# Moving the last 64 rows of a weight matrix from the start of a decode kernel to its tail, in eight 8-row DMAs, and filling TensorE's waits there

## The chip, the cores and the metric

The kernel runs on one core of a Trainium2 chip. The metric is the device time of one execution in microseconds (us), as the median of several runs. The profile is one more execution under the hardware profiler. Its span, from the first to the last instruction, is some 1.5 us shorter than the device time.

Beside the views that are quoted below, the trace records the start and length of every DMA packet and the arrival of every DMA completion. Neither record names the DMA engine.

## The reference, cut to what matters

One decode step of a transformer layer for four sequences: attention over a cache of 4096 positions, 32 heads of 128, then a small MLP with a Mish activation. Almost all bytes are the K and V caches, each 4 x 32 x 4096 x 128 bf16.

```python
h  = x + attention(layernorm(x), k_cache, v_cache, wq, wo)
h1 = layernorm(h) @ w1 + b1                      # w1: 640 x 1728
y  = h + (h1 * tanh(softplus(h1))) @ w2          # w2: 1728 x 640
```

1728 is 13 blocks of 128 rows and 64 rows over. These last 64 rows of w2, 80 KB, are what the change moves.

## The kernel before

Each engine has its own program, written by hand with semaphores. SyncE issues all large loads. The loads at the start (cut):

```python
def first_loads():
    load(sp, slot["C"][:, 0 : DC * H * Dh], A_wq..., "wq", "WQ")     # 5 MB
    load(ac, x_bf[:, :], x_rows[:, :], "x", "X")                      # ScalarE's queue
    load(ac, w2_tail[0:FT, :], B_w2[FM * P : F, :], "w2t", "WT")      # 64 rows x 1280 B
    k_load(0)                                                         # 8 MB each
    k_load(1)
# ScalarE's program then starts with the two small b1 loads:
    load(ac, b1r..., "b1a", "B0"); load(ac, b1e..., "b1b", "B1")
```

At the end SyncE issues six pieces of wo, three of w1 and four of w2. TensorE's tail (cut) multiplies each piece as it lands:

```python
wo_mm(2); wo_mm(3)                                # last attention projection
pe.need("ysum"); mm(m_ps, ...); pe.need("sq"); mm(sq_ps, ...)         # layernorm sums
pe.need("cen")
for c0, c1 in ((0, 2), (2, 4), (4, 5)):           # three pieces of w1
    pe.need(("w1", c0))
    ...  mm(h1_w[...], w, cen[:, c, :].unsqueeze(1).to_broadcast([P, WD, N]), ...)
pe.need("act")                                    # VectorE, ScalarE: Mish
pe.need("w2t"); w2_mm(FM)                         # the last 64 rows
for j0, j1 in ((0, 4), (4, 8), (8, 12), (12, 13)):
    pe.need(("w2", j0)); ...  w2_mm(j)
```

N is 4, the number of sequences. WD is 16: each vector of four columns is streamed 16 times over, 64 columns, only to keep TensorE busy. The extra 60 columns are thrown away.

The softmax here doesn't subtract the row's maximum and nothing guards it: scores larger than these inputs give would overflow.

## Time and profile before

| | before |
|---|---|
| device time, median of 3 | 661.71 us (661.27 to 662.37) |
| profiled span | 659.9 us |
| bytes moved | 283.48 MB, mean 430 GB/s |
| busy: VectorE, TensorE, ScalarE | 62%, 58%, 6% |
| last two w2 pieces land (completion records) | 656.98 and 657.39 us |

These lines are from the first parts of the profile's page: busy us of each engine, then the span in 40 slices, with the busy share of the 16 DMA engines in tenths and their rate.

```profile
PE 382.4 (58%) x2630; PEld 68.6 (10%) x1672; DVE 407.7 (62%) x257; ACT 40.7 (6%) x157; POOL 1.7 (0%) x12
...
DMA  9999999999999999999999999999999999999997
GB/s 387 445 445 441 434 406 437 442 441 434 430 417 445 437 437 433 437 417 445 433 441 433 437 417 445 433 437 438 433 421 445 429 437 441 433 421 445 415 416 324
DMA packets 6905, 283.48 MB, mean 430 GB/s; under 512 B 809, under 2 KB 1136, under 8 KB 2160
```

No compute engine is near full, but the DMA engines are at nine tenths or more in every slice except the last. The kernel is a stream of 283 MB, and it ends when the last bytes have landed and been used.

The next lines are from the DMA view of the kernel before: destination and source, issuing queue, count, KB each, and us from issue to landing.

```profile
slotC<-in_A_wq_dram SPq DMA_DIRECT2D x1, 5120.0 KB, 16.0
...
w_tail<-in_B_w_dram ACTq DMA_DIRECT2D x1, 80.0 KB, 13.3
```

The chain of waits that ended last, at its end (start, us, what):

```profile
639.18 17.80 DMA slotA<-in_B_w_dram
656.98 0.04 issue
657.02 0.68 PE red L728 x20
657.70 0.02 issue
657.73 0.32 DVE o_bf L724
```

SyncE has issued the piece at 639.18 us, and 17.80 us pass until it lands: it stands behind other loads in the queue. Then come twenty matmuls, a copy and the store. That is all of the tail that is not DMA. By their single records the last four of the twenty start at 657.43 us, 0.04 us after the last piece has landed. So it is the last landing that counts, though the chain names the piece before it.

The timeline of the kernel before, in its last 7 us, with matmul (PE) and VectorE (DVE) lines only; in brackets is the idle time ahead of an instruction and what ended it.

```profile
651.32 1.64 PE L728 MATMUL red<-cen,slotB 128*64 128x64 bf16 x28 [0.78 <-DMA slotB<-in_B_w_dram]
...
652.99 1.08 PE L728 MATMUL red<-cen,slotB 128*64 128x64 bf16 x14
...
655.65 0.22 DVE L717 SCALAR_TENSOR_TENSOR act<-tb,hm 128x56 bf16<-128x56 f32 x1
...
656.09 0.72 PE L728 MATMUL red<-slotA,act 128*4 128x160 bf16 x32
...
657.02 0.65 PE L728 MATMUL red<-slotA,act 128*4 128x160 bf16 x20 [0.21 <-DMA slotA<-in_B_w_dram]
```

TensorE waits for w1 before the first line, and for w2 before the last. The activation (`act`) is ready at 655.87 us, 1.1 and 1.5 us ahead of the last two w2 pieces. The windows view shows TensorE's clock in that tail: busy us of PE, PEld, DVE, ACT and POOL with counts, then granted clock, DMA share and GB/s.

```profile
650.00:652.00 2.00, 1.22 (x31) 1.05 (x28) 0.23 (x3) 0.78 (x1) 0.00 (x0) 0.94 1.03 423
652.00:654.00 2.00, 2.00 (x38) 1.81 (x34) 0.00 (x0) 0.00 (x0) 0.00 (x0) 0.50 1.03 423
654.00:655.00 1.00, 0.83 (x42) 0.64 (x40) 0.74 (x4) 0.25 (x1) 0.00 (x0) 0.50 0.99 396
...
656.00:657.00 1.00, 0.81 (x36) 0.52 (x34) 0.00 (x0) 0.00 (x0) 0.00 (x0) 1.00 0.38 146
```

The clock halves from 652 to 655 us and is full again by the last w2 matmuls.

### The profile page before, as it was taken

Reading aid. Unit: us, or ns where it says so; the run is one execution under the profiler, and the core shown is the slowest. Engines: PE = TensorE matmul, PEld = TensorE weight load, DVE = VectorE, ACT = ScalarE, POOL = GpSimd, SP = SyncE. Lnnn points to the kernel's source line nnn. Section 1 sums busy time; section 2 is a strip of 40 time slices with the busy share of each in tenths; the row PEclk is TensorE's granted clock in tenths of the full one; section 3 lists DMA queues with packets and bytes.
Section 4 is the critical chain, followed back from the end, with each engine's and each line's share of the span. In section 5 each row is a group of like instructions: output and inputs, shape, how many; then the busy total and the mean of one; then the engine's idle time right before and its main releaser. Section 6 shows DMA issues by size and latency. Waiting matters only on the chain. (4 is left out here: it accounts for less than half of the span.)

```text
span 659.9 us, 4968 instructions
## 1 busy us (share of the span) xinstructions
PE 382.4 (58%) x2630; PEld 68.6 (10%) x1672; DVE 407.7 (62%) x257; ACT 40.7 (6%) x157; POOL 1.7 (0%) x12
## 2 busy tenths in 40 slices
PE   0356758556317595738417485848434757675766
PEld 0100000101101010101100010010110001010145
DVE  1077988495049778757208798849306798857702
ACT  0200000000000000000000000000000000000011
POOL 0000000000000000000000000000000000000000
PEclk9768787979759697958767888788875879796968
DMA  9999999999999999999999999999999999999997
GB/s 387 445 445 441 434 406 437 442 441 434 430 417 445 437 437 433 437 417 445 433 441 433 437 417 445 433 437 438 433 421 445 429 437 441 433 421 445 415 416 324
DMA packets 6905, 283.48 MB, mean 430 GB/s; under 512 B 809, under 2 KB 1136, under 8 KB 2160
## 3 DMA queue, kind: packets, MB, share of 16 engines
q1 hardware_dynamic: 6784, 283.27, 99.4%
q8 instruction: 6, 0.10, 0.1%
q10 hardware_dynamic: 112, 0.09, 0.0%
q14 instruction: 3, 0.02, 0.0%
HBM read 283.35 MB, written 0.01 MB: 429 GB/s over the span
## 5 line engine op out<-in xcount | busy, mean ns | idle before, releaser
L527 DVE TENSOR_TENSOR slotA<-slotA,q_bc 128x8192 bf16<-128x8192 bf16 x32 | 140.6, 4415 | 92.2 <-DMA slotA<-in_A_k_cache_dram 92.2
L527 DVE TENSOR_TENSOR slotB<-slotB,q_bc 128x8192 bf16<-128x8192 bf16 x32 | 140.7, 4416 | 16.2 <-DMA slotB<-in_A_k_cache_dram 16.2
L538 DVE TENSOR_REDUCE s_f<-red 128x64 f32<-128x1024 f32 x64 | 78.0, 1219 | 96.4 <-PE red L738 96.3
L738 PE MATMUL red<-slotA,ident 128*128 128x512 bf16 x480 | 137.3, 450 | 0.0
L738 PE MATMUL red<-slotB,ident 128*128 128x512 bf16 x480 | 124.5, 418 | 0.0
L728 PE MATMUL red<-slotA,ident 128*128 128x512 bf16 x32 | 14.5, 452 | 128.5 <-PEq L49 128.5
L728 PE MATMUL pv<-slotC,e 128*32 128x512 bf16 x768 | 51.9, 430 | 39.6 <-PEq L49 36.6
L728 PE MATMUL red<-slotB,ident 128*128 128x512 bf16 x32 | 14.0, 437 | 86.9 <-PEq L49 86.9
L404 ACT ACTIVATE ex<-s_f 128x64 bf16<-128x64 f32 x64 | 16.4, 256 | 511.4 <-DVE s_f L538 511.4
L552 DVE TENSOR_TENSOR e<-ex,hmask 128x512 bf16<-128x512 bf16 x64 | 39.8, 683 | 0.0
L728 PEld LDWEIGHTS pv<-slotC,e 128*32 128x32 bf16 x768 | 22.3, 107 | 97.7 <-issue 83.6
L728 PEld LDWEIGHTS red<-slotA,ident 128*128 128x128 bf16 x32 | 3.2, 99 | 197.2 <-issue 197.1
L728 PEld LDWEIGHTS red<-slotB,ident 128*128 128x128 bf16 x32 | 3.1, 98 | 169.0 <-issue 169.0
L728 PEld LDWEIGHTS o_ps<-pv_sb,selo 128*32 128x32 f32 x136 | 13.5, 109 | 63.6 <-issue 63.5
L728 PE MATMUL o_ps<-pv_sb,selo 128*32 128x128 f32 x136 | 18.0, 276 | 0.0
L728 PE MATMUL pv<-slotA,e 128*32 128x512 bf16 x256 | 14.5, 379 | 0.9 <-PEq L49 0.9
L414 ACT COPY pv_sb<-pv 128x512 f32<-128x512 f32 x16 | 9.4, 585 | 70.6 <-PE pv L728 70.6
L404 ACT ACTIVATION_READ_ACCUMULATOR ex<-s_f 128x1 f32 x64 | 11.9, 186 | 0.0
L577 DVE RECIPROCAL rl<-misc 32x1 f32<-32x1 f32 x4 | 0.6, 151 | 14.4 <-PE misc L728 14.4
L728 PEld LDWEIGHTS pv<-slotA,e 128*32 128x32 bf16 x256 | 7.1, 97 | 22.2 <-issue 16.6
L517 DVE CAST b1T<-pv 128x13 bf16<-128x13 f32 x1 | 0.2, 174 | 13.1 <-PE pv L728 13.1
L728 PE MATMUL red<-slotC,lnT 128*32 128x512 bf16 x40 | 4.4, 620 | 6.0 <-PEq L49 6.0
(105 smaller groups left out, 70.3 us busy)
## 6 DMA issues: line engine op xcount, KB each, us to landing
slotC<-in_A_v_cache_dram SPq DMA_DIRECT2D x2, 4096.0 KB, 40.5
slotC<-in_A_wq_dram SPq DMA_DIRECT2D x1, 5120.0 KB, 16.0
slotB<-in_A_wo_dram SPq DMA_DIRECT2D x3, 1280.0 KB, 17.7
slotA<-in_B_w_dram SPq DMA_DIRECT2D x3, 640.0 KB, 18.9
slotB<-in_B_w_dram SPq DMA_DIRECT2D x2, 864.0 KB, 24.4
slotB<-in_A_wo_dram SPq DMA_DIRECT2D x1, 640.0 KB, 21.4
slotB<-in_A_wo_dram SPq DMA_DIRECT2D x1, 480.0 KB, 22.1
slotB<-in_B_w_dram SPq DMA_DIRECT2D x1, 432.0 KB, 22.8
```

The costliest lines, as they stand in the source:

```text
L404: lambda: a.activation(out=ex[:, sl], in_=s_f[:, sl], func=ACT.Exp, scale=SCALE, accum_out=rs[:, b, s : s + 1],),
L414: lambda: a.copy(out=pv_sb[:, :, :].rearrange("p r d -> p (r d)"), in_=pv[:, :]),
L517: dv.do(lambda: v.tensor_copy(out=b1T[:, 0:FM], in_=b1_ps[:, 0:FM]), "b1m", DV)
L527: lambda: v.tensor_tensor(out=t, in0=t, in1=q_bc[:, hg, b, :].unsqueeze(1).to_broadcast([P, RS, Dh]), op=ALU.mult,),
L538: lambda: v.tensor_reduce(out=s_f[:, s * RS : (s + 1) * RS], in_=red[:, k : k + 2, :].rearrange("p k (r c) -> p (k r) c", c=CW), axis=AX.X ...
L552: lambda: v.tensor_tensor(out=e[:, sl, :], in0=ex[:, sl].unsqueeze(2).to_broadcast([P, RS, G]), in1=hmask[:, :].unsqueeze(1).to_broadcast( ...
L577: dv.do(lambda: v.reciprocal(out=rl[:, :], in_=l_ps), ("rl", hg), DV)
L728: lambda: nc.tensor.matmul(out_, lhsT=lhsT, rhs=rhs, start=start, stop=stop, skip_group_check=skip),
L738: return t.add_instruction(mybir.InstMatmult(name=nc.get_next_instruction_name(), engine=mybir.EngineType.PE, ins=[t.lower_ap(rhs), t.lowe ...
```

## The change

The intent has two parts. The DMA part takes the 80 KB out of the start and puts them between w1 and w2, in eight DMAs of eight rows, each row four partitions from the next. The TensorE part streams 4 columns instead of 64 for the second and third w1 piece, and adds eight matmuls of zeros in waits, to keep the clock up.

```diff
@@ first_loads
-        load(ac, w2_tail[0:FT, :], B_w2[FM * P : F, :], "w2t", "WT")
@@ sync_prog, after the three w1 pieces
+        for k in range(FT // 8):
+            r = slice(k // 4 * 32 + k % 4, k // 4 * 32 + 32, 4)
+            load(sp, w2_tail[r, :], B_w2[FM * P : F, :][r, :], ("w2t", k), "WT")
@@ pe_tail
+        def busy(n):
+            for _ in range(n):
+                mm(o_full[:, :], ident[:, :], zeros[:, 0:1].to_broadcast([P, 512]), True, True)
@@ before pe.need("ysum"), before pe.need("cen"), before pe.need("act")
+        busy(1)
+        busy(3)
+        busy(4)
@@ w1 matmuls
+                    wd = WD if c0 == 0 else 1
-                        h1_w[0 : (P if j < FM else FT), j, :, :], w,
-                        cen[:, c, :].unsqueeze(1).to_broadcast([P, WD, N]), False, done,
+                        h1_w[0 : (P if j < FM else FT), j, 0:wd, :], w,
+                        cen[:, c, :].unsqueeze(1).to_broadcast([P, wd, N]), False, done,
@@ before w2_mm(FM)
-        pe.need("w2t")
+        pe.need(("w2t", FT // 8 - 1))
```

## The prediction

> **What bounds the kernel now: the 16 DMA engines, throughout.** The page gives a DMA share of 9 tenths or more in every slice but the last, 283.48 MB at 430 GB/s over 659.9 us; by stretches the share is 1.00 from 2 to 600 us and 0.99 to 655 us. The trace's DMA records show each engine's packets back to back until the last w2 piece. VectorE (62%), TensorE (58%) and ScalarE (6%) have slack. The chain that ended last is the queue issuing weight pieces, 17.80 us of DMA for w2, 0.68 us of matmuls, 0.32 us of VectorE and the store. The last w2 pieces land at 656.98 and 657.39 us.
>
> **Removed, added, moved.**
> - The 80 KB of w2's last 64 rows (64 packets of 1280 B) go from the start, on all 16 engines, to between w1 and w2. The Trainium skill ("DMA: Bandwidth & Descriptors", Why a DMA increments its semaphore by 16 and not by 1) says that a DMA uses the largest engine count up to 16 that divides the slowest dimension, and the lowest-numbered engines: eight rows use engines 0 to 7 only. So engines 8 to 15 lose four packets of 55 ns, about 0.21 us; engines 0 to 7 get eight instead of four, about 0.27 us more with semaphore writes. No trace shows yet which engines lag: the 16 completions of the last w2 piece spread over 1.69 us. If the laggards are among 8 to 15, the end comes 0.2 us sooner; if among 0 to 7, up to 0.27 us later.
> - Between 6 and 12 us, while the early w2 rows pass, wq packets took up to 1646 ns instead of 1514, about 0.3 us per engine. If those rows cause it, that comes back.
> - Eight more DMA issues on SyncE before w2's, some 0.43 us each. The last w2 issue has over 14 us of lead: no gap in the DMA.
> - w1's later 42 matmuls stream 4 columns instead of 64. They took 1.64 us (28) and 1.08 us (14, clock 0.50). I expect about 1.4 and 0.6 us, and the activation some 0.4 us sooner (before: 655.87 us).
> - Eight zero products of 512 columns, 0.22 to 0.43 us each by the spacings in this trace, fill waits: after y (0.38 us), before cen (0.7 us), before act (1.1 us). Cold, they can overrun by up to 0.7 us; what follows waits for w1 and w2 pieces. The clock should stay at 1.0 from about 648 us; before, it fell to 0.50 at 652 to 655 us.
>
> **On the critical path.** Only the last landing plus some 2.5 us (matmuls, copy, store). TensorE was already at full clock there (1.00 from 656 us), so the warm-up saves nothing visible. The move gives between -0.5 and +0.3 us.
>
> **Predicted: 661.4 us, range 660.6 to 662.2** (before: 661.27 to 662.37). Faster by over 2%: 0.005; within 2%: 0.985; slower: 0.01.
>
> **What would show it.** DMA share and bytes unchanged; last w2 landing within 0.5 us of 657.4; w2's last rows landing near 653 us; wq packets at 1514 ns throughout; matmuls on w1's later pieces shorter; activation earlier, then TensorE waiting for w2; the chain still ending in w2's DMA.
>
> **What would make it wrong.** Small DMAs filling the queue's rings so that w2's issues come too late; zero products cold and behind the last landing; a displaced instruction fetch.

## The result

| | before | changed |
|---|---|---|
| device time, median of 6 | 661.74 us (661.23 to 662.37) | 661.52 us (661.30 to 661.76) |
| ratio | 1 | 0.9997 (0.9984 to 1.001) |
| profiled span | 659.9 us | 660.0 us |
| wq has landed | 16.01 us | 15.38 us |
| third w1 piece has landed | 652.35 us | 651.91 us |
| activation ready | 655.87 us | 654.54 us |
| last w2 piece has landed | 657.39 us | 657.57 us |

Ratios are the mean time of one kernel's fast runs over that of the other's fast runs of the same rounds, so they are not quite the ratio of the medians. Landings are the last of a DMA's 16 completion records, counted from the start of the span. The result is the same within noise. The lower rows show that this is not because nothing happened: the DMA stream gained 0.63 us at the start, still had 0.44 us of it at the third w1 piece, and was 0.18 us behind at the end. These are single profiles. A repetition of the changed kernel (`e11_changed_again` below) was 0.33 and 0.17 us ahead and 0.13 us behind at these places. In the ten profiles without early rows wq landed between 15.18 and 15.68 us, in the two with one early 64-row DMA at 16.01 and 16.14. The activation came 1.33 us sooner, which bought nothing.

The page of the changed kernel, then its DMA view:

```profile
PE 383.8 (58%) x2636; PEld 68.4 (10%) x1680; DVE 407.8 (62%) x257; ACT 40.7 (6%) x157; POOL 1.7 (0%) x12
...
DMA  9999999999999999999999999999999999999997
...
DMA packets 6954, 283.50 MB, mean 430 GB/s; under 512 B 857, under 2 KB 1184, under 8 KB 2208
```

```profile
slotC<-in_A_wq_dram SPq DMA_DIRECT2D x1, 5120.0 KB, 15.4
...
w_tail<-in_B_w_dram SPq DMA_DIRECT2D x8, 10.0 KB
```

The stream is as full as before, and wq takes 15.4 instead of 16.0 us. The end of the chain that ended last, in the changed kernel:

```profile
642.29 14.90 DMA slotA<-in_B_w_dram
657.19 0.04 issue
657.23 0.65 PE red L730 x20
657.89 0.02 issue
657.91 0.32 DVE o_bf L726
```

The issue came 3.1 us later, because of the eight issues ahead of it, but there were still 14.90 us to the landing: the queue never ran dry. What follows the landing takes as long as before. The timeline of the changed kernel:

```profile
650.85 1.15 PE L730 MATMUL red<-cen,slotB 128*64 128x4 bf16 x28 [0.66 <-DMA slotB<-in_B_w_dram]
...
652.03 0.71 PE L730 MATMUL red<-cen,slotB 128*64 128x4 bf16 x14
...
653.49 1.49 PE L730 MATMUL o_ps<-zeros,ident 128*128 128x512 bf16 x3 [0.21 <-DMA w_tail<-in_B_w_dram]
...
654.32 0.22 DVE L719 SCALAR_TENSOR_TENSOR act<-tb,hm 128x56 bf16<-128x56 f32 x1
...
657.23 0.62 PE L730 MATMUL red<-slotA,act 128*4 128x160 bf16 x20 [0.83 <-DMA slotA<-in_B_w_dram]
```

The w1 matmuls are shorter and the activation is earlier, and the gain turns into a longer wait: 0.83 instead of 0.21 us ahead of the last twenty matmuls. The windows view of the changed kernel shows the clock:

```profile
650.00:652.00 2.00, 1.34 (x38) 1.21 (x35) 0.00 (x0) 0.47 (x1) 0.00 (x0) 1.00 1.05 407
652.00:654.00 2.00, 1.79 (x60) 1.43 (x59) 1.03 (x5) 0.25 (x1) 0.00 (x0) 0.84 1.00 410
654.00:655.00 1.00, 1.00 (x7) 0.15 (x5) 0.51 (x2) 0.00 (x0) 0.00 (x0) 0.50 0.99 394
...
656.00:657.00 1.00, 0.41 (x15) 0.07 (x4) 0.00 (x0) 0.00 (x0) 0.00 (x0) 0.61 0.34 116
```

The fall of the clock was put off, not prevented: by the trace's clock records it lasted from 651.75 to 655.16 us in before and from 653.37 to 656.79 us here, 3.41 us in both. The last four zero products come as it begins: their first weight load starts at 653.21 us.

### The profile page after: what moved, and what is told of

The parts are those of the page before. It is cut to its first block, busy times and chain, and to the rows that moved or that the text cites. A ratio compares the mean times of both kernels' runs of the same rounds, so it can differ in the third digit from the quotient of the medians.

```text
span 660.0 us, 4989 instructions
## 1 busy us (share of the span) xinstructions
PE 383.8 (58%) x2636; PEld 68.4 (10%) x1680; DVE 407.8 (62%) x257; ACT 40.7 (6%) x157; POOL 1.7 (0%) x12
## 5 line engine op out<-in xcount | busy, mean ns | idle before, releaser
L740 PE MATMUL red<-slotB,ident 128*128 128x512 bf16 x480 | 126.1, 422 | 0.0
L730 PE MATMUL red<-slotB,ident 128*128 128x512 bf16 x32 | 14.2, 443 | 89.1 <-PEq L49 89.1
L730 PE MATMUL y_ps<-a_t,slotB 128*128 128x64 bf16 x160 | 7.3, 211 | 0.0
## 6 DMA issues: line engine op xcount, KB each, us to landing
slotC<-in_A_wq_dram SPq DMA_DIRECT2D x1, 5120.0 KB, 15.4
slotB<-in_A_wo_dram SPq DMA_DIRECT2D x3, 1280.0 KB, 15.4
```

The costliest lines, as they stand in the source:

```text
L730: lambda: nc.tensor.matmul(out_, lhsT=lhsT, rhs=rhs, start=start, stop=stop, skip_group_check=skip),
L740: return t.add_instruction(mybir.InstMatmult(name=nc.get_next_instruction_name(), engine=mybir.EngineType.PE, ins=[t.lower_ap(rhs), t.lowe ...
```

## The experiments

Theory A: the slowest of the 16 DMA engines ends the kernel, and TensorE's tail is hidden behind its last landing. Rival B: TensorE's tail matters, and the DMA move gives its gain back. Rival C, for the tail of the DMA stream: the number of issues or the bytes cost the time, not which engine moves them. A fourth reading, D, came out of the first four runs. All results were correct to the check, `e9_unloaded` included: the comparison's tolerance does not notice the rows that it leaves out.

### Each part alone

`e1_pe_only` is the kernel before with only the TensorE part:

```diff
+        load(ac, w2_tail[0:FT, :], B_w2[FM * P : F, :], "w2t", "WT")     # early again, one DMA
-        for k in range(FT // 8): ...                                      # no DMAs between w1 and w2
```

> The w2 rows stay in one early 64-row DMA; only the 4-column streaming and the eight zero products are added to the kernel before. Theory A (the slowest DMA engine ends the kernel; TensorE's tail is hidden behind w2's landing): activation about 1.3 us earlier than before's 655.87 us, as in the changed kernel (654.54), but the last w2 landing stays at 657.4 us (within 0.15) and the time at that of before, within 0.2 us. Rival B (the warm TensorE is what makes the tail, and the DMA move takes it back): 0.5 to 1 us faster than before. wq lands at 16.0 us as in before in both.

Measured: 661.55 us, ratio to before 0.9997 (0.9984 to 1.0011); last w2 landing 657.53 us. Its timeline:

```profile
654.98 0.22 DVE L717 SCALAR_TENSOR_TENSOR act<-tb,hm 128x56 bf16<-128x56 f32 x1
...
656.13 1.91 PE L728 MATMUL red<-slotA,act 128*4 128x160 bf16 x52
```

The activation came 0.67 us sooner (655.20 us), half of what I expected, and the kernel was not faster. By subtraction, the other half of the 1.33 us in the changed kernel goes with w1's earlier landing. Rival B falls in its simple form. Something of it is true, though: in this profile the clock fell to 0.50 at 652.49 us and stayed there to the end, the 52 matmuls on w2 ran on without a pause, and the last one ended 0.51 us behind the last w2 landing instead of 0.28 in before.

`e2_move_only` is the changed kernel without the zero products and with 64 columns everywhere:

```diff
-        busy(1)
-        busy(3)
-        busy(4)
-                    wd = WD if c0 == 0 else 1
+                    wd = WD
```

> Only the w2 rows move (eight 8-row DMAs between w1 and w2); 64 columns everywhere and no zero products. Theory A: wq lands at 15.4 us (0.6 us sooner than before), the third w1 piece about 0.4 us sooner, the last w2 piece at 657.6 us as in the changed kernel; time equal to the changed kernel within 0.2 us. Rival B: slower than the changed kernel by 0.5 to 1 us, since TensorE is wide and cold.

Measured: 661.66 us, ratio to before 0.9999 (0.9985 to 1.0012). wq landed at 15.32 us, the third w1 piece at 651.91, the last w2 piece at 657.56: the landings of the changed kernel, within 0.06 us. The landings come from the DMA part alone, and the TensorE part buys no time clear of the noise on top of it. Here too the clock was 0.50 at the end, from 649.84 us on:

```profile
655.91 2.13 PE L730 MATMUL red<-slotA,act 128*4 128x160 bf16 x52
```

From the last w2 landing to the end of the span it is 2.67 to 2.69 us in the four profiles with half the clock at the end (this one, `e1_pe_only`, `e3_one64`, `e4_four_rows`), and 2.47 to 2.48 us in the nine with the full clock there, `e8_busy24` left out. So half the clock costs 0.2 us at the end. Whether it is at half there does not follow from the zero products: before, without them, was at full clock, and `e1_pe_only` and `e3_one64`, with them, were not. Within each record the changes of the clock lie whole multiples of 3.413 us apart (in before the stretches last 6.827, 3.413, 13.653 us and so on), and at other times in each run. So a single profile can't tell what moved a fall.

`e8_busy24` measures how much of TensorE's tail is free, with 24 instead of 4 zero products ahead of the activation wait:

```diff
-        busy(4)
+        busy(24)
```

> The changed kernel with 24 instead of 4 zero products ahead of the activation wait: it measures the slack of TensorE's tail. Theory A (TensorE is hidden behind w2's landing): the 20 added products take 20 x 0.22 us warm to 20 x 0.43 us cold, of which some 2.3 us are free (last products of the changed kernel end near 654.9 us, the last w2 pieces land at 657.2 and 657.6), so the time grows by 2.5 to 4 us, the last w2 landing stays at 657.6 us and TensorE then waits for no w2 piece. Rival B (TensorE's tail is on the critical path): the time grows by the whole 4.4 us or more.

Measured: 664.10 us (663.38 to 665.21), ratio to before 1.0037 (1.0022 to 1.0053); last w2 landing 657.57 us. Its timeline:

```profile
653.23 5.40 PE L730 MATMUL o_ps<-zeros,ident 128*128 128x512 bf16 x24
...
658.72 1.07 PE L730 MATMUL red<-slotA,act 128*4 128x160 bf16 x52
```

No matmul on w2 waits for a DMA any more, so here TensorE is the critical path. The first matmuls on w2 began at 658.56 us, 3.66 later than in the changed kernel (654.90), but the profiled span grew only from 660.0 to 662.0 us. So 1.7 us of the delay were free. Of these, 0.83 us are the wait ahead of the last twenty matmuls in the changed kernel. The rest comes from the clock, which was 1.00 throughout this tail: all 56 matmuls on w2 took 1.24 us from the first start to the last end, where the first 36 alone took 1.50 us at 0.50 in the changed kernel. The unprofiled time grew more, by 2.7 us over the changed kernel of the same rounds, inside the 2.5 to 4 us expected. Theory A holds for the changed kernel: its fillers are still short of the point where they cost anything.

### Where the gain of the start went

`e3_one64` sends the moved rows in one DMA at the same place:

```diff
-        for k in range(FT // 8):
-            r = slice(k // 4 * 32 + k % 4, k // 4 * 32 + 32, 4)
-            load(sp, w2_tail[r, :], B_w2[FM * P : F, :][r, :], ("w2t", k), "WT")
+        load(sp, w2_tail[0:FT, :], B_w2[FM * P : F, :], "w2t", "WT")
```

> The changed kernel, but the moved rows go in one 64-row DMA on all 16 engines, four packets each, at the same place. Theory A: all engines pay about 0.25 us instead of engines 0 to 7 paying 0.6, so the last w2 piece lands 0.3 to 0.4 us sooner than in the changed kernel, at 657.2 us, and the spread of its 16 completions goes back from 2.3 us to about 1.8; time 0.3 us under the changed kernel. Rival C (the loss in the tail is the queue's eight extra issues or total bytes, not engines): landing as in the changed kernel if bytes, 0.6 sooner if issues.

Measured: 661.87 us, ratio 1.0002 (0.9989 to 1.0016); last w2 landing 657.83 us, 0.26 later than the changed kernel instead of 0.3 to 0.4 sooner. A miss: spreading the rows over 16 engines made the landing later. In its profile another 0.2 us of the time comes from TensorE's clock, which was at half at the end.

`e4_four_rows` uses sixteen DMAs of four rows, sixteen partitions apart:

```diff
-        for k in range(FT // 8):
-            r = slice(k // 4 * 32 + k % 4, k // 4 * 32 + 32, 4)
+        for k in range(FT // 4):
+            r = slice(k, FT, FT // 4)
```

> The changed kernel, but the moved rows go in sixteen 4-row DMAs, which by theory A use engines 0 to 3 only, sixteen packets each, about 1.2 us. If the late engine that the eight-row form hit is among 4 to 7, the last w2 landing falls to about 657.0 us, 0.55 us sooner than in the changed kernel, with the spread at 1.8 us; if it is among 0 to 3, the landing goes to about 658.2 us, 0.6 us later. Rival C (issues): landing later by the cost of eight more issues, with all 16 completions shifted alike.

Measured: 663.68 us, ratio 1.003 (1.0016 to 1.0044); last w2 landing 659.74 us, 2.2 us later than the changed kernel. A miss in size. Four completions of the last w2 piece came 1.78, 2.07, 2.83 and 4.20 us after the first, the other twelve within 1.57 us. So it hit a few engines, at most four, and not all alike, as rival C would have it for issues. But one engine lost far more than the 1.2 us of sixteen packets.

The reason stands in the packet records. I counted packets that took over 2 ns more than the usual length for their size, and summed the excess. The window is 650 to 654 us, for the early forms 4 to 20 us:

```text
kernel            where the 64 rows go                         slowed  excess, us in sum
before            early, one 64-row DMA                           105      5.4
e1_pe_only        early, one 64-row DMA                            99      8.1
changed           tail, 8 x 8 rows, four partitions apart           8      1.4
e3_one64          tail, one 64-row DMA                            201      9.7
e4_four_rows      tail, 16 x 4 rows, sixteen apart                150      8.9
```

The small packets slow the packets of other loads, in the early form too: in before, wq packets of 40,960 bytes took up to 1647 ns from 6 to 12 us, and 1514 ns in the changed kernel. The changed kernel's row order avoids nearly all of it. (A small part of such counts has another cause: in `e9_unloaded` below, which loads none of these rows, one packet is 0.35 us too long, the one that starts as a fetch of instructions ends.) That gives reading D. By the Trainium skill ("SBUF — State Buffer", Door 1: The DMA port swizzle) partitions 4i to 4i+3 and 32+4i to 32+4i+3, for i from 0 to 7, share one DMA port, and by "DMA: Bandwidth & Descriptors" (The descriptor swizzle) these eight partitions are the ones that engine i writes in a 128-partition load. In the eight DMAs of the change row i of each goes to one of exactly these partitions. Neither page says which rows an engine takes of a smaller DMA issued from SyncE or ScalarE, and no record shows it. If each engine takes its equal share of the rows in order, each engine of the change writes to one port, its own. In the 64-row DMA engines 8 to 15 then write partitions 32 to 63, which are the ports of engines 0 to 7, and in the 4-row form each engine writes to four ports.

`e5_contiguous` tests this with one change, the order of rows:

```diff
-            r = slice(k // 4 * 32 + k % 4, k // 4 * 32 + 32, 4)
+            r = slice(8 * k, 8 * k + 8)
```

> The changed kernel with one difference: each 8-row DMA takes eight adjacent rows instead of every fourth row of a half. Theory D (after the 64-row and 4-row runs: what the small packets cost depends on whether an engine writes its own SBUF port; a neighbour's port slows everyone's packets): packets from 650 to 654 us slowed by 5 us or more in sum over the engines (changed kernel 1.4, 64-row run 9.7, 4-row run 8.9), the last w2 landing 0.3 to 1.5 us later than the changed kernel's 657.57, time 0.3 to 1.5 us longer. Rival (count of packets and engines decide, rows don't): same landing and time as the changed kernel within 0.2 us.

Measured: 662.12 us (661.97 to 662.29); last w2 landing 658.19 us, 0.62 later than the changed kernel; 130 slowed packets with 7.2 us of excess. Its timeline shows when the last twenty matmuls could start:

```profile
657.83 0.65 PE L730 MATMUL red<-slotA,act 128*4 128x160 bf16 x20 [0.78 <-DMA slotA<-in_B_w_dram]
```

The number of DMAs, rows, packets and bytes is that of the changed kernel. All five runs are slower than all six of the changed kernel (661.30 to 661.76), though these are from other rounds. So the row order alone is worth 0.6 us here. That the cause is the port, and not the source side of the copy, is argued and not shown, since the trace names neither engine nor port, and the edit reorders the reads together with the writes. `e7_half_rows` below speaks for it: it reads the same contiguous 80 KB from all engines at once, as `e3_one64` does, but to 128 partitions, and there is almost no slowing. But its packets are also half as long, so that the size of the packets remains a rival.

`e9_unloaded` leaves the 64 rows out and uses zeros for them:

```diff
-        for k in range(FT // 8): ...
+        po.do(lambda: g.memset(w2_tail[:, :], 0.0), "w2z", "PO")
```

> Wrong result on purpose: the last 64 rows of w2 are not loaded at all, zeros stand for them. The ceiling of any placement. Theory A: last w2 landing at 656.95 us (third w1 piece 651.9 plus 5.05 as in before), spread 1.7 us, time 0.5 to 0.7 us under before. Rival (80 KB at 430 GB/s, spread over all engines, is all there is): 0.19 us under before.

Measured: 660.83 us (660.76 to 660.98), ratio 0.9983 (0.9969 to 0.9996); last w2 landing 657.03 us, 0.36 us sooner than before and 0.54 sooner than the changed kernel. This is the ceiling, as far as these runs show: by the landings no placement of these rows wins more than about 0.5 us over the changed kernel, by the medians (from other rounds) 0.6 to 0.7.

Where the changed kernel's 0.54 us goes is seen from the 16 completions of the last w1 piece ahead of the moved rows and of the last w2 piece behind them, in ns after the first of each:

```text
before,  third w1:  0  79  81  92 115 204 467 515  663 1037 1271 1426 1464 1512 1551 1689
before,  last w2:   0  96 105 115 165 477 529 645  995 1290 1387 1465 1523 1563 1595 1688
changed, third w1:  0 113 124 151 158 192 212 256  604 1076 1460 1676 1703 1730 1800 1830
changed, last w2:   0  74 567 585 725 792 956 966 1029 1289 1516 1570 1657 1665 2210 2331
```

In before, the spread stays as it was. In the changed kernel the early group has thinned out: of eight completions within 0.26 us of the first, two are left. And two engines now come at 2.21 and 2.33 us, past the old limit of 1.83. The simplest reading is that an engine that was late and also got small packets became the last. The records do not name it, so this is not shown; a repetition of the changed kernel had two late ones too, at 2.30 and 2.31 us.

That eight rows make a DMA of eight engines is seen in the completion records. The Trainium skill ("DMA: Bandwidth & Descriptors", Why a DMA increments its semaphore by 16 and not by 1) says that the sequencer writes the part of unused engines at once and each used engine adds one. The eight 8-row DMAs left 72 records, nine each, and the sixteen 4-row DMAs 80, five each; a 64-row DMA left 16. The trace agrees with the page.

### Early or late

`e6_early_own` puts the eight DMAs, with their row order, back at the start:

```diff
         load(ac, x_bf[:, :], x_rows[:, :], "x", "X")
+        for k in range(FT // 8):
+            r = slice(k // 4 * 32 + k % 4, k // 4 * 32 + 32, 4)
+            load(ac, w2_tail[r, :], B_w2[FM * P : F, :][r, :], ("w2t", k), "WT")
```

> The changed kernel, but the eight every-fourth-row DMAs go back to the start, on ScalarE's queue, where before had its one 64-row DMA. Theory D: nearly no slowed packets from 4 to 20 us (before 5.4 us in sum), the last w2 landing near 657.5 us and the time as in the changed kernel within 0.2 us, since the engines never idle and the place of the 80 KB does not matter. Rival (early is bad in itself): slowed packets and wq at 16.0 us as in before.

Measured: 666.11 us, ratio 1.0059 (1.0045 to 1.0073), last w2 landing 662.14 us. Far off, but no packet was slowed from 4 to 20 us, and wq landed at 15.28 us. The timeline of this run shows why:

```profile
0.73 5.34 ACTq L263 DMA_DIRECT2D w_tail<-in_B_w_dram  x8
...
7.51 0.26 ACTq L263 DMA_DIRECT2D b1r<-in_B_b_dram  x1
...
44.12 0.26 PE L730 MATMUL pv<-ident,b1r 3*128 3x3 bf16 x4 [22.90 <-PEq L49]
...
44.58 0.33 SPq L263 DMA_DIRECT2D slotC<-in_A_v_cache_dram  x1
```

The 3 KB of b1 were issued behind the eight small DMAs on the same queue and were not used until 44.12 us (21.04 in the changed kernel). VectorE's first multiply and SyncE's first V load waited for that, and from 70 to 80 us the DMA share fell to 0.89. It says nothing of the row order: the experiment had a second cause in it.

`e10_early_b1_first` takes that cause out:

```diff
         load(ac, x_bf[:, :], x_rows[:, :], "x", "X")
+        load(ac, b1r[:, :], ..., "b1a", "B0")
+        load(ac, b1e[:, :], ..., "b1b", "B1")
+        for k in range(FT // 8): ...                     # as in e6
```

> The early eight-DMA form again, but with the two small b1 loads issued ahead of the eight, since in the first try they queued behind them, b1 came at 44 us and the first V load was issued at 44.6 instead of 21.5 us. Theory D: no slowed packets, the first V load issued near 21.5 us, K and V loads as in the changed kernel, last w2 landing 657.5 us and time within 0.2 us of the changed kernel: with rows at their own ports, early or late does not matter. Rival (early is bad in itself): 0.3 us or more slower than the changed kernel.

Measured: 661.19 us (661.14 to 661.73), ratio 0.9991 (0.9977 to 1.0004), beside the changed kernel's 661.39 (`e11_changed_again`) in the same rounds; last w2 landing 657.27 us. The last of the eight DMAs landed only at 44.17 us, and up to 45 us there was no more slowing than in the changed kernel without any early rows (20 packets and 0.13 us in sum, against 27 and 0.15). With rows in this order early is no worse than late; the landing was even 0.25 us sooner, which I did not expect and can't tell from the spread between single profiles. So the move as such is not what matters. That the row order decides in the early place too is likely but not shown: no run put adjacent rows into eight early DMAs.

> The changed kernel unaltered, for the same rounds as the others: 661.5 us, last w2 landing 657.6 us, spread of its 16 completions 2.3 us.

Measured: 661.39 us (661.38 to 661.70), ratio 0.9992 (0.9979 to 1.0006); last w2 landing 657.52 us, spread 2.31 us. As expected.

### A version that beats both

`e7_half_rows` splits each row in two, so that 64 rows of 1280 bytes become 128 of 640 bytes, on 128 partitions in one DMA. It left 16 completion records, so all 16 engines carry it, eight half rows each if they share alike. Partition 2f+h then holds half h of row f. The activations of the 64 rows are doubled by one matmul with a selection matrix and masked by the parity of the partition; this happens while TensorE would wait for w2 anyway.

```diff
-        for k in range(FT // 8): ...
+        load(sp, w2_tail[:, :], B_w2[FM * P : F, :].rearrange("f (h c) -> (f h) c", h=2), "w2t", "WT")
+        # setup: pairs[f, p] = 1 where p // 2 == f; parity[p, h] = 1 where p % 2 == h
+        mm(rep_ps, pairs..., act[0:FT, FM, :], True, True, "rep")          # after pe.need("act")
+        v.tensor_tensor(out=act2, in0=rep_ps (twice), in1=parity, op=ALU.mult)
-        w2_mm(FM)                                                          # ahead of the four pieces
+        w2_mm(FM)   # ahead of the last piece, with act2[:, k // 2, :] and w2_tail[:, k % 2 * OC : ...]
```

> A candidate to beat both: the 64 rows as 128 half rows of 640 bytes in one 128-partition DMA[...]; activations of these rows are doubled by a selection matmul and masked by parity, once, off the critical chain. Theory D: few slowed packets, each engine pays about 0.25 us (estimate: eight packets of some 30 ns) instead of 0.6 on engines 0 to 7, so the last w2 landing comes at 657.2 us, 0.35 sooner than in the changed kernel, time 661.2 us. Rival C: as the 64-row run, 657.8 us.

Measured: 661.09 us (660.98 to 661.44), ratio to before 0.9988 (0.9974 to 1.0002); last w2 landing 657.12 us; three slowed packets, of which the one behind an instruction fetch makes 0.35 of 0.38 us. A packet of 640 bytes took 32 ns. In its timeline the doubling costs nothing, and the last w2 pieces still end the wait:

```profile
655.00 0.18 PE L755 MATMUL misc<-act,pairs 64*128 64x4 bf16 x1
...
655.23 0.17 DVE L744 TENSOR_TENSOR act<-misc,parity 128x8 bf16<-128x8 f32 x1 [0.74 <-PE misc L755]
...
656.76 0.45 PE L755 MATMUL red<-slotA,act 128*4 128x160 bf16 x16 [0.41 <-DMA slotA<-in_B_w_dram]
```

`e12_half_again` is the same kernel in the rounds of `e11_changed_again`:

> The half-row form again, beside the changed kernel in the same rounds. Theory D: 0.3 to 0.5 us under the changed kernel, every run under its median; last w2 landing 657.1 us. If the first result was chance: within 0.1 us of it.

Measured: 661.07 us (660.95 to 661.15), ratio to before 0.9986 (0.9973 to 1.0); last w2 landing 657.13 us. Each of its five runs was faster than each of the changed kernel's five (661.38 to 661.70). Mean over mean of these same rounds, 661.06 over 661.47, is 0.9994. It lies 0.1 us in landing from the ceiling of `e9_unloaded`. It is a gain of 0.3 us by the medians and 0.4 by the means in 661, far below the 2% that counts as faster. Against before, each of the five runs is faster than all nine of the same rounds (661.48 to 662.99), while the interval of the ratio just reaches 1.

The forms side by side (the medians are from four sets of rounds), without `e6_early_own` and `e8_busy24`; landings in us from the start of the span:

```text
kernel               wq     3rd w1   last w2   median   ratio to before
before               16.01  652.35   657.39    661.74   1
e1_pe_only           16.14  652.48   657.53    661.55   0.9997
changed              15.38  651.91   657.57    661.52   0.9997
e11_changed_again    15.68  652.18   657.52    661.39   0.9992
e2_move_only         15.32  651.91   657.56    661.66   0.9999
e3_one64             15.21  652.58   657.83    661.87   1.0002
e5_contiguous        15.46  652.50   658.19    662.12   1.0002
e4_four_rows         15.48  652.32   659.74    663.68   1.003
e10_early_b1_first   15.53  652.21   657.27    661.19   0.9991
e7_half_rows         15.34  651.90   657.12    661.09   0.9988
e12_half_again       15.52  651.90   657.13    661.07   0.9986
e9_unloaded          15.52  652.02   657.03    660.83   0.9983
```

## Why the prediction was right

It predicted 661.4 us, and 661.52 was measured, inside the range and within 2% of before. Its steps:

- **The DMA stream bounds the kernel.** Right. The share and the bytes did not change, the chain still ends in w2's DMA, and `e1_pe_only` and `e2_move_only` show that neither part alone moves the time. `e8_busy24` shows that TensorE's tail could start 1.7 us later at full clock without cost. What the step left out is that half the clock at the end costs 0.2 us.
- **The start gives back what the early rows cost.** Right. Slowed wq packets vanished, and wq landed 0.63 us sooner: 0.21 us of packets and about 0.3 us of slowing had been named, 0.51 in all. The prediction left open whether the rows cause the slowing. `e3_one64` and `e5_contiguous` show that they do, and that the order of rows decides.
- **The tail pays between -0.2 and +0.27 us by which engines are late.** Right in kind: the last landing went from 657.39 to 657.57 us, +0.18, inside the -0.5 to +0.3 named for the whole move. The size fits too: engines 0 to 7 were to end with "about 0.27 us more" for eight packets than for four, which with four packets of 55 ns is 0.49 us against no packets; against the landing in `e9_unloaded` two profiles of the changed kernel say 0.54 and 0.49 us. That the last engines are among 0 to 7 fits this, but the records name no engine.
- **Eight more issues leave no gap.** Right: 14.90 us from issue to landing in place of 17.80. The moved rows landed at 653.26 us (predicted: near 653). The prediction feared a displaced instruction fetch. The changed kernel has one more fetch of 16 KB than before, at 656.82 us, and it did not delay the landing: `e2_move_only` does not have it, and w2 lands at 657.56 us there.
- **w1's matmuls get shorter.** 1.15 and 0.71 us, against 1.4 and 0.6 predicted. The activation came 1.33 us sooner, not 0.4: I had not added w1's earlier landing, 0.44 us, nor the full clock under the bias and h matmuls between 651 and 653 us.
- **The clock stays at 1.0 from 648 us.** Wrong. It held to 653.37 us and was 0.50 until 656.79; the weight loads of two neighbouring zero products there start at 653.49 and 653.91 us, 0.42 us apart, where in `e8_busy24` a product took 0.22 on average (5.40 us for 24). The Trainium skill ("TensorE: Matmul & The Clock Gate", Part 1) says that the clock is set by how busy TensorE has been recently. TensorE was busy for 1.34 of the 2 us from 650 to 652, in matmuls of 4 columns, and waited for the second piece of w1. That the fall came of this is not shown: it began 1.6 us later than in before, but its time differs from run to run (652.20 us in the repetition), and no run varies this stretch alone. It cost nothing, since the clock was back at 1.00 before the last twenty matmuls.

The prediction was thus right for the reason it gave. The number alone would say little: the forecast gain of 0.3 us is smaller than the spread of before's own runs (661.23 to 662.37), and the range of 1.6 us holds the time of before as well. It is the landings, the chain and the two part kernels that bear the steps out. What it did not see is that the odd row order of the change is its most valuable part: adjacent rows would have cost 0.6 us more.

## What to carry to other kernels

In a kernel that is bound by DMA throughout, moving a load in time gives nothing by itself; what counts is the load of the engine that ends last, and small rows written to few partitions can slow the loads around them (130 to 201 packets here). Give such a remainder to all 128 partitions in one DMA if the arithmetic can be bent to it, and else try the order of rows: here rows four partitions apart did best, and that this keeps each engine at its own port is the likely reason. Starting TensorE's work sooner in a tail where it waits for the last weights bought nothing here, and its clock at the very end was worth 0.2 us, so look first at what ends the last wait.

## What the Trainium skill lacked or had wrong

- No page gives a figure for what the order of rows in a DMA of few partitions costs other loads ("DMA: Bandwidth & Descriptors" would be the place). Here eight DMAs of eight adjacent rows slowed 130 packets by 7.2 us in sum and landed w2 0.62 us later than eight DMAs with rows four partitions apart (8 packets, 1.4 us).
- The same page's table, Latency and other measured facts, names two engines that are usually slower, and puts that down, as a guess, to DMAs issued from GpSimd. It has no figure for how far the engines of one load end apart. In this kernel, with loads from SyncE and ScalarE only, the 16 completions of a late load are spread over 1.69 us (before), half of them more than 0.9 us behind the first.
- "Runtime: NRT & Kernel Launch" (Instruction fetch mechanics) calls the cost of fetching a 16 KiB block of instructions mostly hidden. That is said of the engine that fetches; beside a full stream of loads the fetch takes DMA time: in before a 16,384-byte packet on the instruction queue lasted 0.89 to 1.0 us, and the 65,536-byte packet that began as it ended 2.89 to 2.92 us instead of 2.42 (packet records).
- No page gives a time for what a small load loses behind other small loads of its own queue beside a full stream: eight early 8-row DMAs ahead of the 3 KB of b1 on ScalarE's queue put off its use from 21.04 to 44.12 us.
